# Late attention scores from rounded parts, one PSUM bank for two early results, layer 1 started four slots earlier, products three steps behind

## The chip, the cores and the metric

The kernel runs on one core of a Trainium2 chip. The time is that of the whole program in device microseconds (us), median of three runs. Engines are called as the profile calls them: PE is TensorE (PEld its weight loads), DVE is VectorE, ACT is ScalarE, POOL is GpSimd, and SP is the engine whose queue issues nearly all DMAs.

## The reference

Block-causal attention (4 batches, 8 heads, 576 positions of 64 values, blocks of 64), whose output goes through two feed-forward layers.

```python
scores = scale * np.matmul(q, k.transpose(0, 1, 3, 2))
mask = block_i >= block_j
scores = np.where(mask, scores, -1000000000.0)
scores = scores - np.max(scores, axis=-1, keepdims=True)
attn = np.exp(scores)
attn = attn / (np.sum(attn, axis=-1, keepdims=True) + 1e-09)
x = np.matmul(attn, v)                        # to (2304, 512)
h = x @ w_in                                  # 512 -> 2048, layer 1
x = (np.maximum(h, 0.0) + alpha * np.minimum(h, 0.0)) @ w_out
h = x @ w_in2                                 # layer 2
y = np.where(h > 0.0, h, np.exp(np.minimum(h, 0.0)) - 1.0) @ w_out2
```

Here `scale` is 0.125. Everything is 32-bit on input and output.

## The kernel before

**Pairs and slots.** Two heads of one batch make a pair; there are 16. A pair's 576 queries are cut into tiles: queries 0 to 255 are one early tile (i = 0), and 256 to 383, 384 to 511 and 512 to 575 (of both heads) are the late tiles i = 2, 3 and 4. The attention runs in 64 slots, one tile in each, in an order written out by hand: slots 0 to 15 are the early tiles of pairs 0 to 15, slots 16 to 63 the late tiles, three slots a pair. In slot k `scores` puts q times k of its tile in one of two double banks of PSUM (`pair`), `maxima` takes the row maxima on DVE (with a memset for the mask), and `exponentials` runs Exp on ACT. Two slots on `normalise` scales the tile `p` by the reciprocal of its sums, on POOL; three slots on (early) or five (late) PE transposes it and ACT and DVE copy it to `pt`; five (early) or seven slots on `second` multiplies it with v, and ACT and DVE write the result to `x` as a rounded part and the rest. Each engine works through its list in the order in which the program was written, so an instruction that waits holds all behind it on its engine.

**Two kinds of product.** A 32-bit product on PE runs as two instructions in the profile. Elsewhere the kernel takes a number apart into a high part rounded to the matmul's fp32r format and the low rest, and sums three fp32r products, high by high, high by low and low by high (`PASSES`). Before the change the scores are 32-bit products, layers 1 and 2 are threefold fp32r products. The two heads of a pair lie in partitions 0 to 63 and 64 to 127, and their score products use the two halves of the array; tile i = 4 takes both heads at once through `qdiag`, a 128 by 128 block-diagonal matrix of q.

**PSUM banks.** Transposes and the results of `second` take banks in turn from the ring `t`, banks 4 to 7. Once layer 1 begins beside attention the ring has banks 4 to 6, and bank 7 alone holds layer 1's sums (ring `h`).

**Layer 1 beside attention.** Tokens are in five units (512, 512, 512, 512, 256). For units 0 to 2 the first four of 16 slices of the hidden dimension are computed during attention by `l1_beside`: 16 parts of six products each, for every unit first 8 parts of h = x w_in (L523), then 8 of h w_out (L534). The parts are strewn between slots: unit 0 over slots 18 to 33, unit 1 to 47, unit 2 to 71. After the second part of each h, `l1_gate` takes Relu on ACT (`neg`), g on DVE in the next slot behind that slot's maxima, the rounded part on ACT and the rest on POOL (tile `gs`). The weights come as 64-bit halves of 512 KB through `load_w`, which converts them with two ACT, three DVE, a POOL, an ACT and a DVE instruction; slots in `w_slots` start one.

**Afterwards** the rest of layer 1 (units in stages A, B, D) and layer 2 (stage C) run step by step: step i computes h for one slice (L505, L556), and behind it come the output products (L606, L581) of step i - `lag`, with `lag` = 2. g and e have two buffers (tag `g`), h has three banks, the sums have five.

## Time and profile before

| what | value |
|---|---|
| time, median of 3 runs | 1034.4 us (1034.02 to 1036.47) |
| the profiled execution | 1030.47 us, span 1028.7 us, mean granted PE clock 0.988 |
| PE busy | 971.9 us (94%), 4912 matmuls |
| DVE, ACT, POOL busy | 542.3 (53%), 432.4 (42%), 291.6 us (28%) |
| chain that ended last | PE 65%, DVE 11%, DMA 10%, ACT 4%, POOL 4% |

The profiled execution is 0.4% under the median. Busy shares are over the whole span; attention with layer 1 beside it is the first 275 us, where all engines are much in use, and the rest is mostly PE.

### The profile page before, as it was taken

The page shows a single profiled execution, that of the slowest core. Times are in us where ns is not written, and L with a number is a line of the kernel's source. Part 1 is how long each engine was busy: PE and PEld are TensorE (multiplying, and loading weights), DVE is VectorE, ACT ScalarE, POOL GpSimd, SP SyncE. Part 2 cuts the span into 40 slices and gives each one's busy share as a digit, 9 for nine tenths or more (in the row PEclk, how much of TensorE's full clock was granted, in tenths as well). Part 3 has the DMA queues.
Part 4 walks back from the last instruction along what each step waited for, and adds up shares of the span by engine and source line. Part 5 has one row for each costly group of instructions (what it writes and reads, how often), then busy time and mean ns, then how long its engine had stood idle before and what let it go on. Part 6 is the DMA issues. An engine that isn't in the chain of part 4 may idle for free.

```text
span 1028.7 us, 13713 instructions
## 1 busy us (share of the span) xinstructions
PE 971.9 (94%) x4912; PEld 766.2 (74%) x4912; DVE 542.3 (53%) x1070; ACT 432.4 (42%) x953; POOL 291.6 (28%) x344
## 2 busy tenths in 40 slices
PE   6778999999989999999999998999999999999997
PEld 4445666666667877779888886788888888888896
DVE  6886566677476776753213378833333333333343
ACT  6775565576355554543223355422222222222232
POOL 3555254345255545443323344300000000000000
PEclk8999999999989999999999999999999999999999
DMA  6454352633536677545523255202100200200010
GB/s 211 154 200 141 89 143 76 209 103 115 200 107 201 221 234 217 180 155 185 164 82 123 105 191 222 98 1 83 41 1 7 117 1 1 83 1 1 1 42 21
DMA packets 61156, 116.25 MB, mean 113 GB/s; under 512 B 11552, under 2 KB 29984, under 8 KB 59936
## 3 DMA queue, kind: packets, MB, share of 16 engines
q1 hardware_dynamic: 60800, 115.11, 34.2%
q8 instruction: 39, 0.64, 0.3%
q10 hardware_dynamic: 288, 0.26, 0.1%
q14 instruction: 29, 0.24, 0.1%
HBM read 83.89 MB, written 31.46 MB: 112 GB/s over the span
## 4 chain that ended last, share of the span: by engine, by line
PE 65%; DVE 11%; DMA 10%; ACT 4%; issue 4%; POOL 4%; SPq 0%; POOLq 0%; ACTq 0%; DVEq 0%
PE bank L581 18%; PE bank L556 17%; DMA wraw<-w 8%; PE bank L606 6%; PE bank L505 6%; PE bank L390 4%; PE pair L249 3%; POOL wword L142 3%; PE bank L523 3%; PE bank L534 3%; PE bank L336 2%; DVE wword L137 2%; DVE wword L132 2%; DVE wword L133 2%; ACT wword L127 2%
## 5 line engine op out<-in xcount | busy, mean ns | idle before, releaser
L556 PE MATMUL bank<-x,w 128*128 128x512 f32 (+1 forms) x960 | 210.0, 368 | 0.0
L556 PEld LDWEIGHTS bank<-x,w 128*128 128x128 f32 x960 | 169.3, 188 | 31.3
L505 PE MATMUL bank<-x,w 128*128 128x512 f32 (+1 forms) x816 | 175.7, 365 | 1.3 <-DVE xtail L83 1.3
L505 PEld LDWEIGHTS bank<-x,w 128*128 128x128 f32 x816 | 141.5, 189 | 26.1 <-ACT xtail L396 1.4
L561 DVE TENSOR_SCALAR e<-e 128x512 f32<-128x512 f32 (+1 forms) x80 | 31.9, 399 | 172.0 <-ACT e L560 172.0
L560 ACT ACTIVATE e<-bank 128x512 f32<-128x512 f32 (+1 forms) x80 | 44.3, 554 | 184.8 <-PE bank L556 184.8
L142 POOL TENSOR_TENSOR wword<-wword,wraw 128x512 int32<-128x512 int32 x64 | 91.6, 1432 | 91.5 <-DVE wword L137 45.4
L488 DVE SCALAR_TENSOR_TENSOR g<-neg,beta,bank 128x512 f32<-128x512 f32 (+1 forms) x80 | 55.2, 690 | 105.6 <-ACT neg L485 103.6
L581 PE MATMUL bank<-w,gsl 128*128 128x512 f32 x432 | 105.9, 391 | 2.6 <-DVE z L617 1.3
L581 PE MATMUL bank<-w,gs 128*128 128x512 f32 x432 | 105.0, 390 | 1.0 <-DVE gs L83 1.0
L90 POOL TENSOR_SCALAR p<-p,stat 128x128 f32<-128x128 f32 (+4 forms) x144 | 78.0, 555 | 92.1 <-DVE stat L307 69.2
L606 PE MATMUL bank<-gsl,w 128*128 128x512 f32 (+1 forms) x408 | 93.6, 375 | 9.4 <-ACT gsl L492 3.5
L581 PEld LDWEIGHTS bank<-w,gsl 128*128 128x128 f32 x432 | 80.3, 188 | 20.7 <-DVE z L617 2.1
L581 PEld LDWEIGHTS bank<-w,gs 128*128 128x128 f32 x432 | 80.5, 188 | 17.8 <-DVE gs L83 1.5
L83 POOL TENSOR_TENSOR gs<-g,gs 128x512 fp32r<-128x512 f32 (+1 forms) x46 | 58.9, 1280 | 120.5 <-ACT gs L492 113.8
L606 PE MATMUL bank<-gs,w 128*128 128x512 f32 (+1 forms) x408 | 89.1, 366 | 3.0 <-POOL gs L83 3.0
L606 PEld LDWEIGHTS bank<-gsl,w 128*128 128x128 f32 x408 | 71.9, 193 | 26.0 <-ACT gsl L492 4.1
L298 ACT ACTIVATE p<-pair,stat 128x128 f32<-128x128 f32 (+4 forms) x144 | 78.3, 557 | 30.8 <-DVE stat L281 29.0
L606 PEld LDWEIGHTS bank<-gs,w 128*128 128x128 f32 x408 | 70.5, 189 | 16.6 <-POOL gs L83 4.5
L485 ACT ACTIVATE neg<-bank 128x512 f32<-128x512 f32 (+1 forms) x80 | 43.9, 549 | 72.5 <-PE bank L505 69.2
L83 DVE TENSOR_TENSOR w<-wword,w 128x512 fp32r<-128x512 f32 x64 | 58.3, 915 | 26.6 <-ACT w L152 25.6
L270 DVE TENSOR_REDUCE stat<-pair 128x2 f32<-128x256 f32 (+3 forms) x80 | 63.2, 806 | 7.7 <-PE pair L254 5.7
(68 smaller groups left out, 1174.0 us busy)
## 6 DMA issues: line engine op xcount, KB each, us to landing
wraw<-w SPq DMA_DIRECT2D x64, 512.0 KB, 4.1
x<-xd SPq DMA_DIRECT2D x24, 512.0 KB, 6.9
xd<-x SPq DMA_DIRECT2D x4, 2048.0 KB, 7.7
x<-yd SPq DMA_DIRECT2D x4, 2048.0 KB, 8.7
vraw<-v_a SPq DMA_DIRECT2D x24, 256.0 KB, 3.7
zd<-z SPq DMA_DIRECT2D x20, 256.0 KB, 2.8
kraw<-kT SPq DMA_DIRECT2D x16, 288.0 KB, 4.0
yd<-gsl SPq DMA_DIRECT2D x8, 512.0 KB, 4.1
```

Of the source, the lines that this page charges most:

```text
L83: return {"v": dve, "p": pool_e}[eng].tensor_tensor(out=out, in0=x, in1=f32(high), op=ALU.subtract)
L90: return pool_e.tensor_scalar(out, x, 1.0 if scale is None else scale, 1.0, ALU.mult, ALU.mult)
L142: pool_e.tensor_tensor(out=w, in0=w, in1=units, op=ALU.add)
L270: peak = lambda out, x, axis=AX.X: dve.tensor_reduce(out=out, in_=x, axis=axis, op=ALU.max, negate=True)
L298: act.activation(out=out, in_=x, func=AF.Exp, bias=stat[:, k:k + 1], scale=0.125, accum_out=stat[:, SUMS + 2 * k:SUMS + 2 * k + 1])
L485: act.activation(out=neg, in_=h, func=AF.Relu, scale=-1.0)
L488: dve.scalar_tensor_tensor(out=g, in0=neg, scalar=beta[:, f:f + 1], in1=h, op0=ALU.mult, op1=ALU.add)
L505: pe.matmul(h, w_in(0, f, wp_, kc), x[:, xp_, kc, :n], start=kc == 0 and t == 0, stop=kc == KC - 1 and t == 2)
L556: pe.matmul(h, w_in(1, f, wp_, kc), x[:, xp_, kc, :], start=kc == 0 and t == 0, stop=kc == KC - 1 and t == 2)
L560: act.activation(out=e, in_=h, func=AF.Exp)
L581: pe.matmul(acc, gs[:, gp_, tg * P:(tg + 1) * P], w_out(1, f, wp_, 0, DM), start=f == 0 and t == 0, stop=f == NF - 1 and t == 2)
L606: pe.matmul(acc, w_out(0, f, wp_, m * P, P), gs[:, gp_, :n], start=first and t == 0, stop=last and t == 2)
```

## The change

1. Early tiles: q is multiplied by 0.125 in place, once for two pairs (POOL, 128 by 512; the first on DVE in two halves), and the multiplication of the maxima (L281) and the scale of Exp go.
2. Late tiles: `high_parts` (POOL: q times 0.125 rounded, 128 by 320; k rounded, and k minus that, 128 by 576 each), three slots before the pair's first late slot; `low_parts` (one DVE instruction of 128 by 320), two before; `diagonal` fills two matrices, the rounded one on POOL, the low one on ACT. The scores are threefold fp32r products.
3. The result of `second` for an early tile and the smaller of the early tile's two groups of transposes share one bank, so an early slot takes two banks of the ring, not three.
4. Layer 1 beside attention starts at slot 14: unit 0's h parts lie in slots 14 to 22 and its output parts in 22 to 30, unit 1's in 30 to 39 and 39 to 47, unit 2's in 47 to 59 and 59 to 71. The first weight half starts in slot 1 instead of before slot 0, and eight are started by slot 16 instead of 18.
5. `lag` is 3, and g and e have three buffers.

```diff

-    qdiag = [ap1.tile([P, P], F32, name=f"qdiag{i}") for i in range(2)]
-    for t in qdiag:
-        pool_e.memset(t, 0.0)
+    qdiag = [[ap1.tile([P, P], F32R, name=f"qdiag{i}{k}") for k in range(2)] for i in range(2)]
+    for ts in qdiag:
+        for t in ts:
+            pool_e.memset(f32(t), 0.0)

...
         b, p = PAIRS[n]
-        st[n]["q"], st[n]["k"] = q, k = raw_tiles()
+        st[n]["raw"] = q, k = raw_tiles()
         hs = slice(2 * p, 2 * p + 2)
...

+    def high_parts(n):
+        s = st[n]
+        q, k = s["raw"]
+        for which, x, scale in (("q", q[:, 256:], 0.125), ("k", k, None)):
+            s[which] = [ap2.tile([P, x.shape[1]], F32R, tag=f"{which}{t}", name=f"{which}{t}") for t in "hl"]
+            copy("p", s[which][0], x, scale)
+        low_part("p", s["k"][1], k, s["k"][0])
+
+    def low_parts(n):
+        s = st[n]
+        hi, lo = s["q"]
+        dve.scalar_tensor_tensor(out=lo, in0=s["raw"][0][:, 256:], scalar=0.125, in1=f32(hi), op0=ALU.mult, op1=ALU.subtract)
+
     def diagonal(n):
-        for x in range(2):
-            r = slice(64 * x, 64 * x + 64)
-            copy("p", qdiag[n % 2][r, r], st[n]["q"][r, 512:])
+        for low in range(2):
+            for x in range(2):
+                r = slice(64 * x, 64 * x + 64)
+                copy("pa"[low], qdiag[n % 2][low][r, r], f32(st[n]["q"][low])[r, 256:320])

...
         if i < 4:
-            c = 256 * (n % 2) if i == EARLY else 0
-            tiles = [(c + P * j, slice(lo, hi)) for j, lo, hi in EARLY_TILES] if i == EARLY else [
-                (P * i, slice(0, P * (i + 1)))]
-            for q0, cols in tiles:
+            if i == EARLY:
+                c = 256 * (n % 2)
+                for j, lo, hi in EARLY_TILES:
+                    for x in range(2):
+                        r = slice(64 * x, 64 * x + 64)
+                        pe.matmul(sb[:, x, lo:hi], s["q"][r, c + P * j:c + P * j + P], s["k"][r, c:c + hi - lo],
+                                  start=True, stop=True)
+                return
+            q0, cols = P * i - 256, slice(0, P * (i + 1))
+            for t, (qp, kp) in enumerate(PASSES):
                 for x in range(2):
                     r = slice(64 * x, 64 * x + 64)
-                    pe.matmul(sb[:, x, cols], s["q"][r, q0:q0 + P], s["k"][r, c:c + cols.stop - cols.start],
-                              start=True, stop=True)
+                    pe.matmul(sb[:, x, cols], s["q"][qp][r, q0:q0 + P], s["k"][kp][r, cols], start=t == 0, stop=t == 2)
         else:
...
             for r in range(2):
-                pe.matmul(sb[:, r, :kn], qdiag[n % 2], s["k"][:, kn * r:kn * (r + 1)], start=True, stop=True)
+                for t, (qp, kp) in enumerate(PASSES):
+                    pe.matmul(sb[:, r, :kn], qdiag[n % 2][qp], s["k"][kp][:, kn * r:kn * (r + 1)],
+                              start=t == 0, stop=t == 2)

...
             peak(stat[:, 0:1], sb[:, :, :S // 2], AX.XY)
-        dve.tensor_scalar(stat[:, :width(i)], stat[:, :width(i)], 0.125, None, ALU.mult)

...
         for k, (out, x) in enumerate(todo):
-            act.activation(out=out, in_=x, func=AF.Exp, bias=stat[:, k:k + 1], scale=0.125,
+            act.activation(out=out, in_=x, func=AF.Exp, bias=stat[:, k:k + 1],
                            accum_out=stat[:, SUMS + 2 * k:SUMS + 2 * k + 1])
...
             for t, lo, hi in EARLY_TILES:
-                tb, w = bank[take("t")], hi - lo
+                tb, w = (shared.pop() if shared and t == 0 else bank[take("t")]), hi - lo
                 for x in range(2):
...

+    shared = []
+
     def second(n, half):
...
         chunks = range(2 if half == 0 else 5)
-        op = bank[take("t")]
+        if half == 0:
+            shared[:] = [bank[take("t")]]
+            op = shared[0][:, 256:]
+        else:
+            op = bank[take("t")]
         for j in chunks:
...

-    transposes_at, products_at, other_at = {}, {}, {}
+    transposes_at, products_at, other_at, SPLITS = {}, {}, {}, {}

...
         plan(k + 7, lambda n=n: second(n, 1), products_at)
+    def scale_early(d, cols, eng):
+        q = st[2 * d]["q"][:, cols]
+        copy(eng, q, q, 0.125)
+
     for d in range(1, NP // 2):
+        plan(2 * d - 2, lambda d=d: scale_early(d, slice(0, 512), "p"))
         if d > 1:
...
         plan(k - 6, lambda n=n: load_late(n))
+        plan(k - 3, lambda n=n: high_parts(n), SPLITS)
+        plan(k - 2, lambda n=n: low_parts(n))
         plan(k - 1, lambda n=n: diagonal(n))
...
             scores(*here)
+        shared.clear()
         outs = [p() for p in products_at.get(k, ())]
         move = transposes(*transposes_at[k]) if k in transposes_at else None
+        for emit in SPLITS.get(k, ()):
+            emit()
         for emit in NORM.get(k, ()):
...
         neg = gp.tile([P, 512], F32, tag="neg", name="neg", bufs=1)[:, :n]
-        g = gp.tile([P, 512], F32, tag="g", name="g", bufs=2)[:, :n]
+        g = gp.tile([P, 512], F32, tag="g", name="g", bufs=3)[:, :n]
         t = gs_tile()[:, :, :n]
...
                           start=kc == 0 and t == 0, stop=kc == KC - 1 and t == 2)
-        e = gp.tile([P, 512], F32, tag="g", name="e", bufs=2)[:, :n]
+        e = gp.tile([P, 512], F32, tag="g", name="e", bufs=3)[:, :n]
         gs = gs_tile()[:, :, :n]
...
         load_early(1)
+        for half in range(2):
+            scale_early(0, slice(256 * half, 256 * half + 256), "v")
         load_early_v(0)
-        load_w(*halves.pop(0))
         load_alpha()
...
         end_tick()
-        LEAD = 18
-        ends = [33, X_DONE[2], LAST]
-        w_slots = {3, 6, 9, 12, 14, 16, 18}
+        LEAD = 14
+        stretches = [(LEAD, 22, 22, 30), (30, 39, 39, X_DONE[2]), (X_DONE[2], 59, 59, LAST)]
+        w_slots = {1, 3, 6, 8, 10, 12, 14, 16}
         w_slots |= {27 + 5 * i for i in range(8)}
...
                 if k in w_slots:
-                    arrival[0] = 4 if k > 20 else 2
+                    arrival[0] = 4 if k > 21 else 2
                     load_w(*halves.pop(0))
...
         k = LEAD
-        for u, end in enumerate(ends):
-            assert k >= X_DONE[u]
-            parts, n, first = l1_beside(u), 2 * (FA + KC), k
-            for j in range(n):
-                next(parts)
-                to = first + (2 * (j + 1) * (end - first) + n) // (2 * n)
-                slots(k, to)
-                k = to
+        for u, (a, b, c, d) in enumerate(stretches):
+            assert a >= X_DONE[u]
+            parts = l1_beside(u)
+            for first, end, n in ((a, b, 2 * FA), (c, d, 2 * KC)):
+                slots(k, first)
+                k = first
+                for j in range(n):
+                    next(parts)
+                    to = first + (2 * (j + 1) * (end - first) + n) // (2 * n)
+                    slots(k, to)
+                    k = to
         arrival[0] = 2
...
             first_of.setdefault((k, u), i)
-        lag = 2
+        lag = 3
         w_at = {}
```

On PE at slots 14 to 16, before the change (L249 is a score product, L390 the product with v, L329 a transpose; bank_106 is bank 7):

```order
L249 MATMUL pair_101<-kraw,qraw 128x128 x2
L249 MATMUL pair_101<-kraw,qraw 128x256 x2
L390 MATMUL bank_106<-pt,vraw_113 64x256 x2
L390 MATMUL bank_106<-pt,vraw_113 64x128 x2
L329 MATMUL bank_103<-ident,p_568 128x128 x2
L329 MATMUL bank_104<-ident,p_568 128x128 x4
L249 MATMUL pair_102<-kraw,qraw 128x128 x2
L249 MATMUL pair_102<-kraw,qraw 128x256 x2
L390 MATMUL bank_105<-pt,vraw_114 64x256 x2
L390 MATMUL bank_105<-pt,vraw_114 64x128 x2
L329 MATMUL bank_106<-ident,p_608 128x128 x2
L329 MATMUL bank_103<-ident,p_608 128x128 x4
```

And the same place with the change, up to the scores of slot 16 (L560 is a part of layer 1's h, L270 a late score product, kh, kl, qh and ql the rounded and low parts):

```order
L560 MATMUL bank_106<-x_318,w 128x512 x6
L263 MATMUL pair_102<-kraw,qraw 128x128 x2
L263 MATMUL pair_102<-kraw,qraw 128x256 x2
L417 MATMUL bank_105<-pt,vraw_114 64x256 x2
L417 MATMUL bank_105<-pt,vraw_114 64x128 x2
L350 MATMUL bank_105<-ident,p_613 128x128 x2
L350 MATMUL bank_103<-ident,p_613 128x128 x4
L560 MATMUL bank_106<-x_318,w 128x512 x6
L270 MATMUL pair_101<-kh,qh 128x384 x2
L270 MATMUL pair_101<-kl,qh 128x384 x2
L270 MATMUL pair_101<-kh,ql 128x384 x2
```

Parts of layer 1 now stand ahead of slots 15 and 16, the product with v and the first transposes go to the same bank, and three score products stand where one 32-bit product of two instructions stood.

On POOL around slots 13 to 16 before (L90 p is a normalisation, L142 a weight's addition, L90 qdiag the diagonal):

```order
L90 TENSOR_SCALAR p_525<-p_525,stat_123 128x128 x2
L90 TENSOR_SCALAR p_525<-p_525,stat_123 128x256 x2
L142 TENSOR_TENSOR wword<-wword,wraw 128x512
L90 TENSOR_SCALAR p_568<-p_568,stat_124 128x128 x2
L90 TENSOR_SCALAR p_568<-p_568,stat_124 128x256 x2
L90 TENSOR_SCALAR p_608<-p_608,stat_119 128x128 x2
L90 TENSOR_SCALAR p_608<-p_608,stat_119 128x256 x2
```

And with the change:

```order
L90 TENSOR_SCALAR qraw<-qraw 128x512
L90 TENSOR_SCALAR qh<-qraw 128x320
L90 TENSOR_SCALAR kh<-kraw 128x576
L83 TENSOR_TENSOR kl<-kraw,kh 128x576
L90 TENSOR_SCALAR p_573<-p_573,stat_128 128x128 x2
L90 TENSOR_SCALAR p_573<-p_573,stat_128 128x256 x2
L142 TENSOR_TENSOR wword<-wword,wraw 128x512
L90 TENSOR_SCALAR p_613<-p_613,stat_123 128x128 x2
L90 TENSOR_SCALAR p_613<-p_613,stat_123 128x256 x2
L142 TENSOR_TENSOR wword<-wword,wraw 128x512
```

The three instructions of `high_parts` stand ahead of a slot's normalisation, behind the scaling of the last early q.

On PE at the start of stage A before (L505 is h of a step, L606 the output products of an earlier one):

```order
L505 MATMUL bank_2675<-x_2023,w 128x512 x12
L505 MATMUL bank_2676<-x_2023,w 128x512 x12
L505 MATMUL bank_2677<-x_2023,w 128x512 x12
L606 MATMUL bank_2670<-gsl,w 128x512 x3
L606 MATMUL bank_2671<-gsl,w 128x512 x3
```

And with the change (L542 and L643 are the same lines of code):

```order
L542 MATMUL bank_2976<-x_2249,w 128x512 x12
L542 MATMUL bank_2977<-x_2249,w 128x512 x12
L542 MATMUL bank_2978<-x_2249,w 128x512 x12
L542 MATMUL bank_2976<-x_2249,w 128x512 x12
L643 MATMUL bank_2971<-gsl,w 128x512 x3
L643 MATMUL bank_2972<-gsl,w 128x512 x3
```

A fourth h, in the bank of the first, now stands ahead of the first output products, and so it goes on to the end of layer 2.

## Rows read from the trace of the kernel before

**Rows 1.** Windows: stretch, its length, busy time (instructions) by engine, PE clock, DMA.

```profile
0.00:52.18 52.18, 35.37 (x251) 22.71 (x251) 39.25 (x113) 36.44 (x136) 24.64 (x64) 0.87 0.60 187
52.18:67.82 15.64, 12.00 (x86) 7.29 (x87) 13.23 (x37) 13.04 (x44) 7.62 (x19) 1.00 0.66 221
67.82:198.49 130.67, 118.62 (x665) 77.66 (x664) 86.16 (x224) 74.09 (x186) 58.07 (x88) 0.99 0.39 119
198.49:275.26 76.77, 73.76 (x457) 47.92 (x457) 54.17 (x150) 48.35 (x122) 35.57 (x51) 1.00 0.45 142
275.26:1028.70 753.44, 732.15 (x3456) 610.60 (x3456) 349.50 (x549) 260.50 (x468) 165.72 (x125) 0.99 0.30 102
```

**Rows 2.** Waits of PE, 0 to 52.18 us: total, times, longest.

```profile
PE bank L329 <- DVE x L83: 5.0, 4, 1.6
```

**Rows 3.** Waits of PE, 67.82 to 275.26 us.

```profile
PE bank L523 <- DVE g L488: 8.0, 4, 3.7
```

**Rows 4.** Waits of PE, 275.26 us to the end.

```profile
PE bank L606 <- ACT gsl L492: 3.5, 2, 3.0
...
PE bank L581 <- DVE gsl L83: 0.5, 1, 0.5
```

**Rows 5.** Timeline of PE: start, length, line, output and inputs, count [idle before].

```profile
136.81 1.13 PE L254 MATMUL pair<-kraw,qdiag 128*128 128x288 f32 x4
137.77 0.82 PE L336 MATMUL bank<-ident,p 128*128 128x128 f32 x6
...
139.90 0.92 PE L249 MATMUL pair<-kraw,qraw 64*128 64x384 f32 x4
140.74 2.42 PE L390 MATMUL bank<-pt,vraw 128*64 128x320 f32 x20
...
145.50 1.13 PE L249 MATMUL pair<-kraw,qraw 64*128 64x512 f32 x4
146.56 0.66 PE L342 MATMUL bank<-ident,p 128*128 128x128 f32 x4
```

**Rows 6.** Timeline of PE at the start of stage A.

```profile
275.26 8.42 PE L505 MATMUL bank<-x,w 128*128 128x512 f32 x36 [1.27 <-DVE xtail L83]
286.67 0.79 PE L606 MATMUL bank<-gsl,w 128*128 128x512 f32 x1 [2.98 <-ACT gsl L492]
288.02 5.06 PE L606 MATMUL bank<-gsl,w 128*128 128x512 f32 x11 [0.56 <-POOL gsl L83]
292.88 2.42 PE L505 MATMUL bank<-x,w 128*128 128x512 f32 x9
```

**Rows 7.** Timeline of ACT in that stretch.

```profile
280.88 0.67 ACT L128 ACTIVATE wraw<-wraw 128x512 int32<-128x512 uint32 x1 [6.35 <-DMA wraw<-w]
```

**Rows 8.** Timeline of POOL in that stretch.

```profile
285.01 1.26 POOL L83 TENSOR_TENSOR gs<-g,gs 128x512 fp32r<-128x512 f32 x1 [9.66 <-ACT gs L492]
...
288.25 1.41 POOL L83 TENSOR_TENSOR gsl<-g,gsl 128x512 fp32r<-128x512 f32 x1 [0.28 <-ACT gsl L492]
```

**Rows 9.** Timeline of DVE in that stretch.

```profile
286.31 0.75 DVE L488 SCALAR_TENSOR_TENSOR g<-neg,beta,bank 128x512 f32<-128x512 f32 x1 [2.02 <-POOL gs L83]
287.17 3.04 DVE L83 TENSOR_TENSOR w<-wword,w 128x512 fp32r<-128x512 f32 x2
```

**Rows 10.** Groups by line and shape, 0 to 275 us: busy, mean ns, idle before.

```profile
L83 POOL TENSOR_TENSOR gs<-g,gs 128x512 fp32r<-128x512 f32 x12 | 16.0, 1333 | 36.2 <-ACT gs L492 36.1
...
L83 DVE TENSOR_TENSOR w<-wword,w 128x512 fp32r<-128x512 f32 x16 | 12.1, 757 | 2.3 <-ACT w L152 2.3
...
L90 POOL TENSOR_SCALAR p<-p,stat 128x576 f32<-128x576 f32 x16 | 11.9, 746 | 15.8 <-DVE stat L307 12.2 <-DVE pair L277 3.6
...
L281 DVE TENSOR_SCALAR stat<-stat 128x4 f32<-128x4 f32 x16 | 6.1, 383 | 0.6
```

**Rows 11.** Timeline of SP: the late load of pair 6.

```profile
116.10 0.42 SPq L221 DMA_DIRECT2D kraw<-kT  x1
```

**Rows 12.** DMA issues of the page: KB each, us to landing.

```profile
kraw<-kT SPq DMA_DIRECT2D x16, 288.0 KB, 4.0
```

## The prediction

> **What bounds the kernel now.** I read the busy time by stretch first, cut where the program changes: slot 14 begins at 52.18, slot 18 at 67.82, slot 47 at 198.49, and the first product of stage A at 275.26 [rows 1]. From slot 18 to stage A PE is busy 118.62 + 73.76 = 192.4 of 207.4 us, and after that 732.15 of 753.44: PE is the bound from slot 18 on, with 15.1 and 21.3 us of idle time in its row. Before slot 14 it isn't: PE works 35.37 of 52.18 us, DVE 39.25, ACT 36.44, and in slots 14 to 17 DVE 13.23 and ACT 13.04 of 15.64. There a slot is the sum of hand-overs between two nearly full engines. So time comes from three places: PE work that goes, PE idle time that is filled, and early slots that grow or shrink.
>
> The waits of PE name the idle time. In the early slots it is the transposes that wait for DVE to empty a bank, 5.0 us in four times [rows 2]; from slot 18 it is layer 1's h, which waits for g to be read out of its only bank, 8.0 us [rows 3]; in the stages it is the output products that wait for `gs`, in five rows of the view that come to 9.2 us, of which the first and the last are shown [rows 4]; the rest there are waits for DVE to empty sums, which the change leaves alone.
>
> **Late scores.** From start to start the 32-bit scores take 0.96 us (i = 4), 0.84 (i = 2) and 1.06 (i = 3) [rows 5]. The first is 4 instructions of 288 columns, 0.24 each, or 0.83 ns a column. The 64-row tiles have 4 instructions too, but 4 times 384 columns at that rate would be 1.28, so the two heads run beside each other: two deep 0.64, and 0.20 that doesn't stream; for i = 3 0.85 and 0.21. A threefold fp32r product of full height costs 8.42 / 36 = 0.23 us for 512 columns [rows 6], about 0.13 for 288 and 0.16 of streaming for 384. If the heads still run side by side and the 0.20 is paid once a tile, i = 4 becomes 6 x 0.13 = 0.80 (-0.16), i = 2 becomes 0.48 + 0.20 (-0.16), i = 3 0.64 + 0.21 (-0.21): -0.53 a pair, **-8.5** over 16. No row shows fp32r on 64 rows. Lower bound: nothing but streaming, 0.48, 0.64 and 0.80, -0.94 a pair, -15.0. Upper bound: the heads one behind the other, 6 x 0.17 = 1.04 and 6 x 0.23 = 1.36, +0.34 a pair, +5.4. I take the value nearest to how the same tiles run now.
>
> **The splits.** POOL gets per pair a copy of 576 columns, 0.75, one of 320, 0.41 by the same row, and a subtraction of 576, 1.33 x 576/512 = 1.50 [rows 10]: 2.7 us. In the fullest stretch, slot 47 on, POOL works 35.57 of 76.77 [rows 1]; its six pairs or so there add 16, so it stands at some 70%. A normalisation behind the splits has three slots until its transposes in late slots, so it is late for nobody. DVE gets one low part, 0.75 x 320/512 = 0.47 by the g instruction [rows 9], and loses three scalings of maxima; ACT gets two copies of 64 by 64. All of it lies under PE's work; without that cover it would be 2.7 us a pair. The splits read k three slots sooner than the products did. Pair 6's load was issued at 116.10 and takes 4.0 [rows 11, 12], so it lands near 120, and was used at 139.90 [rows 5]; three slots are 3 x 130.67 / 29 = 13.5 us, which leaves 6 us. I put it at 0.
>
> One cost can't be bounded away: DVE and POOL disturb each other. While POOL subtracted at 288.25 [rows 8], two subtractions of weights on DVE took 3.04 us [rows 9], which is 1.5 each against a mean of 0.76 [rows 10]. By the trace that is 0.75 us for each such meeting, and DVE, 54.17 of 76.77 in its fullest stretch [rows 1], has room for that. The Trainium skill (SBUF — State Buffer, Terms) has it that the pair is an exclusive lock for a whole instruction, and that the loser "fully blocks". Taken at its word, any of DVE's instructions with two SBUF inputs could wait out a whole POOL instruction; that is a rival below.
>
> **Early slots, 0 to 13.** DVE loses a scaling of 0.38 us in every slot [rows 10], 5.4 us in all, and the 5.0 us of waits for banks [rows 2] should go, since an early slot takes two banks of four. Against it stand two scalings of q on DVE ahead of the first scores, and one to two more weight halves that now fall ahead of slot 14, on DVE and ACT. DVE's saving about pays for the halves, ACT's share rises. I take **-1**, bounds -4 and +3.
>
> **Slots 14 to 17.** One part of layer 1 stands there now, ahead of slot 18; with the change there are four, each 6 x 0.23 = 1.4 us, so PE goes from 12.00 to 16.2 us in a stretch of 15.64, while DVE takes on two g's and two low parts and ACT two Relus. The fullest engine works 13.23 of 15.64 us, 85% [rows 1]; at that share 16.2 needs 19.1: +3.5, while 4.2 of PE work is gone from behind slot 18: **-0.7**. Bounds: -4.2 if it all fits in, +3 if a slot here loses 1.5 us more to hand-overs.
>
> **Idle time from slot 18 to stage A.** Of its 15.1 us, 8.0 are h waiting for its bank [rows 3], all in the slots in which DVE also converts weights. Half of unit 0's h parts have moved to earlier slots, the weights are through two slots sooner, and unit 1 has 17 slots for its 16 parts instead of 14. I take **-6**; bounds 0 (the wait moves along with the parts) and -10.
>
> **Three steps behind.** Stage A's 36 first products take 8.42 us from 275.26, and the next h begins at 292.88 [rows 6]. At 0.23 us the 48 products until then need 10.9, so 6.7 are lost: ACT, in order, waited until 280.88 for a weight to land [rows 7] before it could take Relu of the first h, so `gs` came from POOL at 285.01 + 1.26 [rows 8], and eleven of the output products behind it ran at 5.06 / 11 = 0.46 us each [rows 6]. With `lag` 3 PE has four h's, 10.9 us, before it needs that `gs`, until 286.2; it is ready at 286.3. The fourth h wants the bank of the first, which g has read by 283 or so. So nearly all of the 6.7 goes. Of the 9.2 us of waits for `gs` 2.98 and 0.56 lie here, and the other 5.7 are short single waits; a step more of slack, 24 products or 5.4 us, covers each. DVE's wait of 2.02 for a g buffer [rows 9] goes with the third buffer. 12.4 in all; I take **-11** for what turns up anew, bounds -4 and that 12.4. What is late next are the sums that DVE empties between units, which stay.
>
> **Sum.** -8.5 - 1 - 0.7 - 6 - 11 = -27.2, against the profiled execution's 1030.47 (span 1028.7): 1003. The median stands 3.9 us above that execution; with the same difference it is 1034.4 - 27.2 = **1007**.
>
> **Rivals.**
> A. The fp32r halves don't overlap: +5.4 in place of -8.5, 1021. For it: no row shows them. Against: the same partitions and banks overlap now.
> B. The landing of a weight holds ACT longer at stage A, and the fourth h waits for its bank as the output products did: the first 6.7 stay, 1014. For it: an idle time of 6.35 us before one ACT instruction. Against: only 3 us more would matter.
> C. The blocked port: three of DVE's two-input instructions a pair each lose 0.8 us to a POOL instruction. A pair is 207.4 / 16 = 13 us now, of which DVE works 71% in its fullest stretch; 2.4 more and the low part's 0.47 would bring it to 12.1 us, as long as PE's work, and the gain from slot 18 on (8.5 + 6) is lost: 1022. By the lock of that page this would come; the rows show the delay, but few meetings.
> D. It ends slower: POOL waits for landings. Each pair's splits stand in POOL's list ahead of normalisations and `gs`, and if loads land late POOL stands still for that time in every pair. With the change a pair is about 13 - 14.5 / 16 = 12.1 us, of which POOL works 35.57 / 76.77 of 13, or 6.0, and 2.7 more, so a wait of up to 3.4 costs nothing; 5.1 a pair makes the pair 1.7 = 27.2 / 16 longer and takes all the gain. At 6.0 the median would be 1034.4 + 16 x 0.9 = 1049. For it: SP issues in order, behind stores that wait. Against: 6 us of room in the load shown.
> E. Several of these at once, within 0.3%.
>
> **Chances.** Forecast 0.57 (its own range 998 to 1017, from the bounds of the terms), A 0.13, B 0.10, C 0.08, D 0.07, E 0.05. A measurement of this kernel can tell 0.3%, 3 us, from no change. Faster: 0.57 + 0.13 + 0.10 + 0.08 = 0.88; same 0.05; slower 0.07. The range goes from 994, where the score, idle and early terms reach their lower bounds (6.5 + 4 + 3 more), to 1023, which takes in A, B and C and leaves out D, E and the ends of the forecast.
>
> **What would show it.** Late scores from start to start at 0.68, 0.85 and 0.80, and the two heads' instructions starting in pairs; slot 14 near 51, slot 18 near 70, stage A's first product near 259; h's waits for g about 3 us; the next h after stage A's first output products without a gap, and waits for `gs` of about 1 us in all the stages; POOL near 70% from slot 47 on. Wrong would be: six score instructions in a row in 1.0 us or more (A), a PE gap after the third or fourth h of stage A (B), DVE near 95% in late slots (C), POOL idle on a DMA of k (D), or slots 14 to 17 of 6 us, which would eat what the earlier start brings.

## The result and the profile after

The changed kernel takes 1019.37 us (median, 1017.45 to 1023.51) beside 1034.21 for the kernel before on the same chip: ratio 0.9858, interval 0.9821 to 0.9896, so 14.8 us faster. That lies in the predicted range of 994 to 1023, but 12 us above the predicted 1007 and 2 us outside the forecast's own 998 to 1017. The profiled execution took 1017.45 us with a span of 1015.7, 13.0 less than before's 1028.7, and the account below is made between these two.

Windows of the changed kernel, cut as in [rows 1]: slot 14 begins at 50.86, slot 18 at 73.70, slot 47 at 189.01, stage A at 264.40.

```profile
0.00:50.86 50.86, 35.82 (x256) 22.59 (x256) 37.08 (x100) 37.91 (x138) 30.30 (x73) 0.97 0.60 187
50.86:73.70 22.84, 17.31 (x109) 11.47 (x109) 18.05 (x44) 16.57 (x51) 19.88 (x31) 0.93 0.60 218
73.70:189.01 115.31, 107.94 (x699) 77.49 (x698) 80.93 (x196) 73.37 (x198) 76.39 (x110) 0.99 0.38 120
189.01:264.40 75.39, 71.09 (x492) 50.47 (x491) 56.10 (x136) 51.81 (x134) 47.86 (x65) 1.00 0.47 151
264.40:1015.70 751.30, 731.39 (x3456) 612.87 (x3456) 351.29 (x549) 260.50 (x468) 163.05 (x125) 0.99 0.30 102
```

Slots 0 to 13 take 1.3 us less than in [rows 1], slots 14 to 17 take 22.84 instead of 15.64, slot 18 to stage A 190.70 instead of 207.44, and the stages 751.30 instead of 753.44. So the gain is made between slot 18 and stage A, part of it is paid back in slots 14 to 17, and the stages, where the largest term of the prediction lay, give 2.1. Of the 16.7 us between slot 18 and stage A, 6.4 are four parts of layer 1 that now stand ahead of slot 18 (three in slots 14 to 17, one at the end of slot 13), and PE's idle time is 11.67 us instead of 15.05.

PE's timeline at late scores (to set against [rows 5]) and at the start of stage A ([rows 6]):

```profile
236.21 0.44 PE L270 MATMUL pair<-kh,qh 64*128 64x384 f32 x2
236.49 0.34 PE L270 MATMUL pair<-kl,qh 64*128 64x384 f32 x2
236.66 0.34 PE L270 MATMUL pair<-kh,ql 64*128 64x384 f32 x2
236.93 2.42 PE L417 MATMUL bank<-pt,vraw 128*64 128x320 f32 x20
...
241.68 0.50 PE L270 MATMUL pair<-kh,qh 64*128 64x512 f32 x2
...
242.58 0.66 PE L363 MATMUL bank<-ident,p 128*128 128x128 f32 x4
...
243.10 0.38 PE L275 MATMUL pair<-kh,qdiag 128*128 128x288 f32 x1
...
243.98 0.82 PE L357 MATMUL bank<-ident,p 128*128 128x128 f32 x6
...
264.40 11.16 PE L542 MATMUL bank<-x,w 128*128 128x512 f32 x48 [1.27 <-DVE xtail L83]
275.40 0.39 PE L643 MATMUL bank<-gsl,w 128*128 128x512 f32 x1
276.39 2.79 PE L643 MATMUL bank<-gsl,w 128*128 128x512 f32 x11 [0.61 <-POOL gsl L83]
279.02 2.88 PE L542 MATMUL bank<-x,w 128*128 128x512 f32 x12
```

From start to start the scores take 0.72 (i = 2), 0.90 (i = 3) and 0.88 us (i = 4; 0.80 to 0.89 over the pairs): 0.12, 0.16 and 0.08 to 0.16 less than before. The two heads' products start in pairs, within 0.01 us of each other. At stage A the four h's run through, and about 0.9 us is lost ahead of the next h where it was 6.7.

Waits of PE from there to the end (total, times, longest), which answer to [rows 4]:

```profile
PE bank L643 <- ACT z L87: 5.3, 1, 5.3
PE bank L643 <- DVE z L650: 4.8, 3, 2.3
PE bank L643 <- DVE zl L89: 1.6, 2, 0.9
PE bank L643 <- DVE zl L650: 1.4, 2, 1.1
...
PE bank L643 <- POOL gsl L83: 0.6, 1, 0.6
```

The 9.2 us of waits for `gs` are down to 0.6. In their place the output products of layer 1 wait 13.1 us for sums (`z`, `zl`) to be emptied. Before, the same waits came to 4.4, nearly all of it in these two rows:

```profile
PE bank L606 <- DVE z L613: 2.5, 3, 1.4
PE bank L606 <- DVE zl L613: 1.7, 2, 1.1
```

The longest of the new waits stands here in PE's timeline, and behind it ACT's and SP's in the same stretch:

```profile
313.32 1.60 PE L542 MATMUL bank<-x,w 128*128 128x256 f32 x12
314.76 0.52 PE L643 MATMUL bank<-gsl,w 128*128 128x256 f32 x3
320.63 1.01 PE L643 MATMUL bank<-gsl,w 128*128 128x256 f32 x3 [5.35 <-ACT z L87]
...
324.15 2.55 PE L542 MATMUL bank<-x,w 128*128 128x256 f32 x12
```

```profile
315.63 0.40 ACT L529 CAST gs<-g 128x256 fp32r<-128x256 f32 x1 [0.87 <-DVE g L525]
317.36 0.66 ACT L127 ACTIVATE wword<-wraw 128x512 f32<-128x512 f32 x1 [1.32 <-DMA wraw<-w]
...
318.60 0.67 ACT L127 ACTIVATE wword<-wraw 128x512 f32<-128x512 f32 x1
...
319.72 0.39 ACT L522 ACTIVATE neg<-bank 128x256 f32<-128x256 f32 x1
319.98 0.59 ACT L87 COPY z<-bank 128x512 f32<-128x512 f32 x1
```

```profile
303.99 3.18 SPq L507 DMA_DIRECT2D x<-xd  x4
309.75 4.44 SPq L117 DMA_DIRECT2D wraw<-w  x2
```

The last products of unit 3 end at 313.5, its first sum was complete even sooner. The copy to z that empties this sum's bank began at 319.98, because in ACT's list two weight halves and a Relu stand ahead of it, and ACT, in order, stood idle for the 1.32 us before 317.36 until the first half landed. That half was issued at 309.75, behind the four loads of the next x, and landed 7.5 us later; the median of these loads is 4.1. PE also loses clock: it is idle from 315.3, the granted clock is 0.50 (the lower level, 1.2 GHz) from 319.5 to 326.3, and the twelve products at 324.15 take 2.55 us instead of 1.60.

The other waits for sums have DVE in ACT's place. It is mostly at work on weights there rather than idle, and in front of five of these waits a bit operation on a weight (L133), 0.43 us as a rule, takes 1.40 to 1.45. One of the five, in PE's and DVE's timelines:

```profile
377.32 3.98 PE L643 MATMUL bank<-gsl,w 128*128 128x512 f32 x9 [1.83 <-DVE z L650]
```

```profile
374.49 1.45 DVE L133 TENSOR_SCALAR wword<-wword 128x512 uint32<-128x512 uint32 x1
...
376.58 0.68 DVE L650 TENSOR_TENSOR z<-bank,z 128x512 f32<-128x512 f32 x1
```

What makes L133 longer is in the last section.

### The profile page after: what moved, and what is told of

Read it like the earlier page. It is cut to its first block, busy times and chain, and to the rows that moved or that the text cites. A ratio compares the mean times of both kernels' runs of the same rounds, so it can differ in the third digit from the quotient of the medians.

```text
span 1015.7 us, 13946 instructions
## 1 busy us (share of the span) xinstructions
PE 963.5 (95%) x5008; PEld 774.9 (76%) x5008; DVE 543.4 (54%) x1024; ACT 440.2 (43%) x985; POOL 337.5 (33%) x401
## 4 chain that ended last, share of the span: by engine, by line
PE 68%; DVE 11%; DMA 9%; POOL 4%; ACT 4%; issue 2%; SPq 1%; POOLq 0%; ACTq 0%; DVEq 0%
PE bank L618 19%; PE bank L593 18%; PE bank L643 9%; PE bank L542 8%; DMA wraw<-w 6%; PE bank L417 3%; POOL wword L142 3%; PE bank L571 3%; DVE wword L137 2%; PE bank L357 2%; PE pair L270 2%; PE bank L560 2%; DVE wword L133 2%; DVE wword L132 2%; ACT wword L127 1%
## 5 line engine op out<-in xcount | busy, mean ns | idle before, releaser
L542 PE MATMUL bank<-x,w 128*128 128x512 f32 (+1 forms) x816 | 176.7, 367 | 1.3 <-DVE xtail L83 1.3
L542 PEld LDWEIGHTS bank<-x,w 128*128 128x128 f32 x816 | 142.7, 191 | 26.2 <-ACT xtail L423 1.4
L142 POOL TENSOR_TENSOR wword<-wword,wraw 128x512 int32<-128x512 int32 x64 | 89.8, 1405 | 92.5 <-DVE wword L137 53.8
L643 PE MATMUL bank<-gsl,w 128*128 128x512 f32 (+1 forms) x408 | 94.6, 379 | 13.7 <-ACT z L87 5.3
L90 POOL TENSOR_SCALAR p<-p,stat 128x128 f32<-128x128 f32 (+4 forms) x144 | 81.3, 579 | 53.9 <-DVE stat L328 43.4
L643 PEld LDWEIGHTS bank<-gsl,w 128*128 128x128 f32 x408 | 72.8, 196 | 30.0 <-DVE z L650 6.3
L643 PE MATMUL bank<-gs,w 128*128 128x512 f32 (+1 forms) x408 | 87.8, 364 | 0.0
L643 PEld LDWEIGHTS bank<-gs,w 128*128 128x128 f32 x408 | 70.6, 189 | 12.2
L83 DVE TENSOR_TENSOR w<-wword,w 128x512 fp32r<-128x512 f32 x64 | 61.0, 957 | 24.5 <-ACT w L152 23.7
```

The source lines that it names most:

```text
L83: return {"v": dve, "p": pool_e}[eng].tensor_tensor(out=out, in0=x, in1=f32(high), op=ALU.subtract)
L90: return pool_e.tensor_scalar(out, x, 1.0 if scale is None else scale, 1.0, ALU.mult, ALU.mult)
L142: pool_e.tensor_tensor(out=w, in0=w, in1=units, op=ALU.add)
L542: pe.matmul(h, w_in(0, f, wp_, kc), x[:, xp_, kc, :n], start=kc == 0 and t == 0, stop=kc == KC - 1 and t == 2)
L643: pe.matmul(acc, w_out(0, f, wp_, m * P, P), gs[:, gp_, :n], start=first and t == 0, stop=last and t == 2)
```

## The experiments

All thirteen times, each as a ratio to the kernel before in its own comparison, with its interval, and the span of its profiled execution:

| kernel | ratio | span, us |
|---|---|---|
| changed | 0.9858 [0.9821, 0.9896] | 1015.7 |
| lag 2 | 0.9878 [0.9861, 0.9895] | 1018.7 |
| start at slot 18 | 0.9901 [0.9885, 0.9918] | 1020.1 |
| 32-bit late scores | 0.9924 [0.9910, 0.9938] | 1024.6 |
| before with lag 3 | 0.9982 [0.9970, 0.9994] | 1031.5 |
| normalisation first | 0.9870 [0.9848, 0.9892] | 1020.3 |
| hand order | 0.9837 [0.9815, 0.9860] | 1015.5 |
| weights' work cut | 0.9781 [0.9758, 0.9803] | 1010.9 |
| third raw buffer | 0.9924 [0.9900, 0.9947] | 1024.7 |
| hand order, A and B | 0.9748 [0.9731, 0.9765] | 1005.8 |
| the same, lag 2 | 0.9806 [0.9787, 0.9826] | 1011.7 |
| two halves later | 0.9890 [0.9870, 0.9911] | 1020.7 |
| g first | 0.9743 [0.9712, 0.9774] | 1007.5 |

0.001 is 1.03 us. The changed kernel's own interval is 4 us wide to either side, so what differs from it by less is read from stretches of the traces. Its profiled execution is the fastest of its four runs, 1.9 us under their median, so a difference of spans can be that much larger than one of ratios for a slower kernel, and that much smaller for a faster one.

**1. The parts alone.** Four kernels. The scaled early q and the shared bank had no run of their own.

```diff
-        lag = 3
+        lag = 2
```

> The changed kernel with the output products two steps behind the first ones again instead of three (the third g buffer stays). First theory: three steps behind removed the 9 us of waits for gs, but waits for the sums between units took their place, so the step was worth about 2 us: 1.5 to 3 us slower than the changed kernel (about 1021), with the waits for gs back at 8 to 10 us and the waits for z down from 13 us to about 4. Rival: the step is worth the 11 us of the prediction and the missing gain is elsewhere: 9 to 12 us slower (about 1029).

```diff
-        LEAD = 14
-        stretches = [(LEAD, 22, 22, 30), (30, 39, 39, X_DONE[2]), (X_DONE[2], 59, 59, LAST)]
-        w_slots = {1, 3, 6, 8, 10, 12, 14, 16}
+        LEAD = 18
+        ends = [33, X_DONE[2], LAST]
+        w_slots = {3, 6, 9, 12, 14, 16, 18}
...
```

> The changed kernel with layer 1 beside attention beginning at slot 18 again, with the old stretches and the old slots for the weight loads. First theory: the start at slot 14 costs 7 us in slots 14 to 17 and gives back about 9 from slot 18 to stage A, so that it is worth 2 to 3 us together with the 1 us ahead of slot 14: the kernel without it is 2 to 4 us slower (about 1022), slots 14 to 17 take 14 to 16 us again. Rival 1: it is worth the 7.7 us of the prediction: 1027. Rival 2: it costs more than it gives back, and the kernel without it is 2 to 5 us faster (about 1015).

```diff
-            for t, (qp, kp) in enumerate(PASSES):
-                for x in range(2):
-                    ...
-                    pe.matmul(sb[:, x, cols], s["q"][qp][r, q0:q0 + P], s["k"][kp][r, cols], start=t == 0, stop=t == 2)
+            q, k = s["raw"]
+            for x in range(2):
+                ...
+                pe.matmul(sb[:, x, :P * (i + 1)], q[r, P * i:P * i + P], k[r, :P * (i + 1)], start=True, stop=True)
...
-        plan(k - 3, lambda n=n: high_parts(n), SPLITS)
-        plan(k - 2, lambda n=n: low_parts(n))
...
```

> The changed kernel with its late scores in 32 bits again, without the splits on POOL, DVE and ACT; everything else as changed. First theory: the shorter scores are worth what their start to start differs, 0.46 us a pair or 7.4 us, and the splits are hidden: 6.5 to 8.5 us slower than the changed kernel (about 1027). Rival: the splits hold up DVE and POOL in the slots in which layer 1's gates and the weights are converted, and eat half of it or more: 0 to 4 us slower (1019 to 1023), with the waits for g and p of slots 18 to 63 down from 10 us to below 6.

The fourth is the kernel before with `lag = 3` and `bufs=3` for g and e.

> The kernel before with the output products three steps behind and three g buffers; nothing else. First theory: about 2 us faster than before (1032), the waits for gs gone and waits for sums between units of 10 us or more in their place. Rival, the prediction's term: 9 to 12 us faster (about 1024).

Lag 2 is 0.0020 above the changed kernel, less than the intervals tell apart, with 7.2 us of waits for `gs` and `gsl` in A, B and D back (8 to 10 had been expected) and those for z and zl there at 4.7. Alone on the kernel before, three steps gain 1.9 us (0.6 to 3.1), and the same waits arise there:

```profile
PE bank L606 <- DVE z L613: 5.3, 3, 2.5
PE bank L606 <- ACT z L87: 5.1, 1, 5.1
```

So the step is worth about 2 us in either kernel, and the rival of 11 falls. The 32-bit scores cost 6.8 us by the ratios; a late pair's three slots, where PE waits for nothing and two parts of layer 1 stand between in both, take 10.36 us with them and 9.90 without, 0.46 x 16 = 7.4. From slot 18 to stage A the 32-bit kernel is only 5.6 us longer, since PE is idle for 10.01 us in it instead of 11.67. So the splits cost at most about 1.7 us there, and the rival, by which they eat half or more, falls on the 6.8 and the 7.4, though the interval of the ratios alone wouldn't exclude it. The start at slot 18 costs 4.4 us: there slot 18 to stage A takes 201.06 us, 10.4 more than with the start at 14 (4.3 of it is idle time of PE, the rest the four parts of layer 1 that then lie there), slots 14 to 17 take 20.08, 2.8 less, and slots 0 to 13 take 48.87, 2.0 less. The first theory expected 14 to 16 us for slots 14 to 17, and that was wrong: even with almost no layer 1 in them they grew by 4.4 over [rows 1]. The waits of PE in them, with the start at 18, point to the splits, since the early normalisations stand behind them on POOL:

```profile
PE bank L350 <- POOL p L90: 4.3, 4, 1.9
```

**2. Slots 14 to 17.** First the order on POOL:

```diff
-        for emit in SPLITS.get(k, ()):
-            emit()
         for emit in NORM.get(k, ()):
             emit()
+        for emit in SPLITS.get(k, ()):
+            emit()
```

> The changed kernel with the normalisations ahead of the splits in POOL's list, in every slot; nothing else. First theory: the splits of pairs 0 and 1 fall in slots 13 and 16, where early normalisations stand behind them that are wanted one slot later, and the chain runs over POOL there: 1.5 to 4 us faster than the changed kernel (about 1016.5), slots 14 to 17 at 19 to 21 us instead of 22.84. Rival: as predicted, nobody waits for POOL behind the splits, slots 14 to 17 are held by DVE and ACT: within 1 us of the changed kernel.

The slots take 22.84 us, as in the changed kernel, and the ratio is 0.9870: the rival held. The 32-bit kernel has no splits at all, and its slots 14 to 17 take 24.34, though its DVE has more to do there (21.32 us against 18.05). With the start at 14 the order of POOL's list isn't what makes these slots long. Then two weight halves out of these slots, `w_slots = {1, 3, 6, 8, 10, 12, 17, 18}`:

> The changed kernel with the two weight halves that are loaded at slots 14 and 16 loaded at slots 17 and 18. First theory: DVE holds slots 14 to 17, and each half costs it 2.3 us there: the four slots shrink from 22.84 us by 3 to 5, and slots 18 to 22 grow by about as much, since DVE is as full there: within 2 us of the changed kernel in all. Rival: PE and the splits make these slots long: they stay at 22 us or more.

They take 22.87 us, while slots 18 to 21 take 22.10 instead of 17.36, and the kernel is 3.3 us slower. The rival's number held; but the conversions that now lie later belonged to slot 16 and after, so of what DVE does in slots 14 and 15 this says nothing. What these slots wait for in the changed kernel is seen in PE's timeline, and below it in DVE's:

```profile
53.94 0.87 PE L417 MATMUL bank<-pt,vraw 128*64 128x256 f32 x8 [2.15 <-DVE pt L89]
...
55.37 1.64 PE L560 MATMUL bank<-x,w 128*128 128x512 f32 x6
...
62.23 1.90 PE L560 MATMUL bank<-x,w 128*128 128x512 f32 x6 [2.75 <-DVE g L525]
```

```profile
57.09 0.56 DVE L243 SCALAR_TENSOR_TENSOR ql<-qraw,qh 128x320 fp32r<-128x320 f32 x1
...
60.49 1.02 DVE L292 TENSOR_REDUCE stat<-pair 128x2 f32<-128x256 f32 x2
61.43 0.74 DVE L525 SCALAR_TENSOR_TENSOR g<-neg,beta,bank 128x512 f32<-128x512 f32 x1
```

The first h is complete at 57.0, g frees its only bank at 62.2, behind 4 us of other work in DVE's list, and the next h holds up the scores behind it in PE's. The last experiment of the series takes g ahead of the maxima (it builds on the hand order of part 3):

```diff
-        if here:
-            maxima(*here)
         after = [h() for h in held]
         held.clear()
+        if here:
+            maxima(*here)
```

> The kernel with ACT's and DVE's lists in the order of the code through the A and B units, and beside attention each g on DVE ahead of the maxima of its slot instead of behind them; nothing else. First theory: what is left of idle time between slot 14 and stage A, 12 us in seven waits of h and of the first output products for g (8.1 and 3.6), comes from g's place in DVE's list, behind 1.2 us of maxima: the seven waits lose about 1 us each, slots 14 to 17 come below 22 us, 3 to 7 us faster than that kernel (about 1003). Rival: the maxima are what the next slots wait for, and g waits for ACT anyway: the waits move to the scores and the transposes, within 2 us or slower.

The waits of h and of the first output products for g fall from 11.7 to 4.9 us, but the slots still take 22.84, with 2.1 us of transposes that wait for POOL and a longer slot 17; the time is the same. The rival held, and ACT's timeline shows one reason. DVE begins the first g at 59.65 instead of 61.43, but ACT's rounding of it stands behind the exponentials of slot 15 and begins when it did, here in the changed kernel and in this one:

```profile
63.34 0.64 ACT L529 CAST gs<-g 128x512 fp32r<-128x512 f32 x1
```

```profile
63.37 0.63 ACT L529 CAST gs<-g 128x512 fp32r<-128x512 f32 x1
```

POOL waits for it and begins the rest of g at 64.06 and 64.08, and behind it in POOL's list stand the splits and the normalisation that slot 17's transposes need. So what DVE's list gives up doesn't get past ACT's and POOL's.

**3. The sums in the stages.** Five kernels test why they are late. In the stages the program fixes the order of PE's list alone; the lists of ACT, DVE and POOL are ordered by the scheduler.

```diff
-    with tc.manual_schedule(engines={ET.PE}):
+    with tc.manual_schedule(engines={ET.PE, ET.Activation, ET.DVE}):
```

> The changed kernel with ACT's and DVE's instructions in the stages in the order in which the code issues them (the scheduler orders only PE's list by hand as it stands); the same instructions, but the emptying of a sum stands behind at most one weight half instead of two. First theory: sums wait for their emptying because it stands in ACT's and DVE's lists behind weights that have just landed or not landed yet; with the other order the waits for z in the A and B units fall from 13 us to below 6, and the kernel is 5 to 9 us faster than the changed one (about 1012). Rival: with three steps behind the two engines have too little time for the sums whatever the order: the waits only move, within 2 us of the changed kernel or slower.

```diff
-            act.activation(out=units, in_=low, func=AF.Copy, scale=2.0 ** -29)
+            if not plain:
+                act.activation(out=units, in_=low, func=AF.Copy, scale=2.0 ** -29)
...
+            if plain:
+                dve.tensor_scalar(w, w, 1.0, 0.001, ALU.min, ALU.mult)
+                return
...
-        later(lead + 1, sign)
-        later(lead + 2, rounded)
+        if not plain:
+            later(lead + 1, sign)
+            later(lead + 2, rounded)
```

(`plain` holds for layer 1's weights in the stages.)

> The changed kernel with a part of the conversion of layer 1's last eight chunks left out in the stages (one of ACT's two reads of the raw words, DVE's sign and POOL's addition; what is left is replaced by a bound and a factor), so that the numbers that come out are other ones. First theory: it is the conversion that holds the emptying of sums: stage waits for z fall from 13 us to below 4, 8 to 12 us faster than the changed kernel (about 1009). Rival: the sums are late for another reason (the bank ring, the stores): z waits stay above 8 us, within 4 us.

```diff
-        raw = wraw_p.tile([P, 2 * DM], U32, tag="wraw", name="wraw")
+        n_w[0] += 1
+        wp, nb = (late_pools[0], 1) if late_pools and n_w[0] % 3 == 0 else (wraw_p, 2)
+        raw = wp.tile([P, 2 * DM], U32, tag="wraw", name="wraw", bufs=nb)
...
-        return late_pools[0].tile([P, 2, 512], F32R, tag="gsl", name="gsl", bufs=4)
+        return late_pools[0].tile([P, 2, 512], F32R, tag="gsl", name="gsl", bufs=3)
```

> The changed kernel with a third buffer for a raw weight half and its word in the stages (and three gsl buffers instead of four, to make room). First theory: the loads of weights are issued only when POOL has added up the half two before, and land behind the loads of x; with a third buffer they are issued some 5 us sooner and ACT no longer stands at a weight that has not landed: the 5.35 us ahead of the emptying of unit 3's sums goes, 3 to 6 us faster (about 1015). Rival: the instructions themselves, not the landing, hold the emptying: within 2 us.

In hand order the A and B units have not one wait of 0.3 us for a sum, but stage C has 11.1 us of waits where it had 0.8 (layer 2's h waits for DVE to read its bank into `e`, 5.3 in five times), so it comes out 2.2 us below the changed kernel, less than the intervals tell apart, between the two theories. Cutting the weights' work gains 8.0 us by the ratios and 4.8 by the spans, and yet the waits for sums stay at 11.5: the longest is 6.41 us, and ACT's rows in front of it are these, with the wait for the landing grown to 4.24:

```profile
319.25 0.66 ACT L127 ACTIVATE wword<-wraw 128x512 f32<-128x512 f32 x1 [4.24 <-DMA wraw<-w]
319.81 0.66 ACT L129 ACTIVATE wraw<-wraw 128x512 int32<-128x512 uint32 x1
```

L129 is the read that the edit leaves out of layer 1's weights, so this weight is one of layer 2's, and whole. The scheduler puts ten halves of layer 2 ahead of stage D. The gain lies behind the A and B units: from D's first product to C's first it takes 197.26 us instead of 202.84, and from A's first to D's first 140.73, no less than in the changed kernel. So less conversion doesn't help the sum that stands behind a load that hasn't landed; this run doesn't say what less conversion of those very weights would do. The third raw buffer gave no answer: with it and one `gsl` less the scheduler's lists came out otherwise, one wait of 7.2 us for a sum arose in C, and it is 6.8 us slower. Then the hand order for A and B alone:

```diff
+    with tc.manual_schedule(engines={ET.PE, ET.Activation, ET.DVE}):
...
+        for i in range(31):
+            step(i)
+
+    with tc.manual_schedule(engines={ET.PE}):
+        for i in range(31, len(steps) + lag):
+            step(i)
```

> The changed kernel with ACT's and DVE's lists in the order of the code up to the end of the A and B units only; the units D and C, where that order had brought new waits of 14 us, are left to the scheduler. First theory: the waits for sums of the A and B units, 10 us (the five of 0.3 us or more up to 402, and what the clock loses behind them), go, and nothing else changes: 7 to 11 us faster than the changed kernel (about 1010). Rival: the waits turn up again later, as they did in C: within 3 us.

> The same with the output products two steps behind. First theory: with the sums emptied in time the third step is worth what the prediction put it at, the waits for gs that it removes: 5 to 9 us slower than the one with three steps (about 1017). Rival: the waits for gs were a matter of ACT's order too, and two steps do as well in that order: within 2 us of the one with three.

With three steps it takes 1007.77 us, 0.0110 or 11.4 us below the changed kernel and 26.1 below the kernel before; it and the one with g first, which builds on it, are the fastest here. ACT's timeline at the same place as above:

```profile
310.94 0.58 ACT L87 COPY z<-bank 128x512 f32<-128x512 f32 x1
311.69 0.59 ACT L87 COPY z<-bank 128x512 f32<-128x512 f32 x1 [0.18 <-PE bank L643]
312.18 0.68 ACT L127 ACTIVATE wword<-wraw 128x512 f32<-128x512 f32 x1
```

The copies of the sums stand ahead of the weight, and PE has no wait there. From stage A's first product to D's first it takes 125.89 us instead of 140.08. But two more things differ in that stretch. ACT takes up 16 weight halves there instead of 24, since those of layer 2 are left for the stages behind; and no L133 is lengthened there, where eight were. So the order of the two lists is what gains; how much of it is the place of the emptying, how much the eight halves and how much the meetings with POOL, these runs don't separate. From there to C's first product it gives 4.9 back, in one wait for a sum between D's first two units, behind two weight halves in DVE's list, so that expectation's "nothing else changes" was too simple:

```profile
453.98 1.01 PE L643 MATMUL bank<-gsl,w 128*128 128x256 f32 x3 [5.92 <-DVE z L654]
```

With two steps in the same order the stretch from A to D takes 128.57 us, against 141.82 for two steps in the scheduler's order, and the whole is 0.0058 or 6.0 us slower, of which the traces show 4.1 from stage A on. So the order takes away the waits for `gs` in A and B too, at two steps all but 1.4 us at stage A's start; the third step is worth 4 to 6 us once the order is right, and about 2 in the scheduler's.

## Why the prediction came out as it did

The direction and the range held, the middle was 12 us too low. That the range held was in part luck: the time lies outside the forecast's own 998 to 1017, and what takes it in is the room that the range left for A, B and C, none of which came in the way that was described. By its own terms, between the two profiled executions:

| term | predicted | measured | how |
|---|---|---|---|
| late scores | -8.5 | -7.4 | 16 x 0.46 |
| slots 0 to 13 | -1 | -1.3 | start of slot 14; the 5.0 of [rows 2] are gone |
| slots 14 to 17 | -0.7 | +0.8 | +7.2, less 6.4 of work gone from behind slot 18 |
| idle time, slot 18 to A | -6 | -3.4 | PE's idle time, 15.05 to 11.67 |
| three steps behind | -11 | -2.1 | stage A to the end |
| sum | -27.2 | -13.4 | spans: -13.0 |

(The median stands 1.9 us above the profiled execution, not 3.9 as the prediction took over from before; that is 2 us of the miss in the other direction.)

**Three steps behind** is the step that was mis-sized, by 9 us. Its mechanism was right as far as it went: the four h's cover the first `gs`, the 6.7 us at stage A became 0.9, and the 9.2 us of waits for `gs` became 0.6. Wrong was the sentence that what is late next, the sums that DVE empties between units, "stay". In the view behind [rows 4] they were a rest of 4.4 us, and I took a small wait for slack. It was small because PE came late: as soon as PE no longer waited for `gs`, it reached the bank of the sum while ACT and DVE were still at, or idle for, the weights in front of it. Going from two steps to three takes these waits from 4.4 to 13.4 us on the kernel before, and going back takes them from 13.1 to 4.7 on the changed one. The order of ACT's and DVE's lists then gives 9.7 us from stage A to the end with the same instructions. [rows 7] held the hint, ACT idle for 6.35 us on a landing, and the prediction used it for one place only.

**Slots 14 to 17** were the second miss, +7.2 in place of +3.5, hidden in the table because four parts of layer 1, 6.4 us, have gone from behind slot 18 and not three: PE's work there came to 17.31 us rather than 16.2, part of it at a lower clock (0.93), and 5.5 us of waits for DVE stand on top. The growth rate from one engine's busy share (85%) was too kind for slots in which three engines hand over to each other and h has one bank. That the slots might take 6 us each was named as what would eat the early start; slots 14 and 15 take 6.08 and 7.12, and against the start at 18 these slots and the ones ahead of them give back 4.8 of the 10.4 us. What bounds them was not settled, beyond the chain from DVE's g over ACT's rounding to POOL that held when g came first: without splits, with the normalisations first, with weights later and with g first they took 24.34, 22.84, 22.87 and 22.84 us.

**Splits at 0**: right for the late slots; POOL works 47.86 of 75.39 us from slot 47 on, 63%, where 70% was forecast. It was wrong in its reason: slots 13 and 16 still hold early normalisations, wanted one slot later and not three, and with the start at slot 18 PE waits 4.3 us for them. With the start at 14 PE doesn't wait for them; that the waits for DVE hide it is likely, not shown.

**Scores**: right within 1.1 us; the 0.16 us of streaming for 384 columns stands in no row, 0.23 us for 512 gives 0.17. **Idle time**: 3.4 of the 6. The waits of h for g between slot 18 and stage A fell from 8.0 [rows 3] to 4.8, not to 3, and those of the output products for g are 3.7. Rival A fell on the pairs, B on the four h's that run through, D on the late slots: none of PE's waits for POOL there is of 0.3 us or more. C did not come in the late slots: DVE stands at 56.10 of 75.39, 74%. But its mechanism, DVE held by POOL, came up in the stages, ahead of the sums.

## What to carry to other kernels

A wait that is small in a profile is not slack: it can be small because the waiting engine came late. Before a wait is priced away, follow the next one in the same engine's list as if the first were gone, and read which instruction stands ahead of its releaser. In an engine's list one instruction that waits for a load holds everything behind it, so short work that frees a bank belongs ahead of work that waits for data. Here a different order of two engines' lists, which also held later weights back, was worth more (11.4 us) than the whole change of distance (about 2).

## What the runs showed of the hardware

DVE and POOL meet in one-input instructions too. In the changed kernel's DVE timeline the bit operation on a weight (L133) takes 1.40 us beside an addition of POOL that had begun 0.37 us sooner:

```profile
423.88 1.40 DVE L133 TENSOR_SCALAR wword<-wword 128x512 uint32<-128x512 uint32 x1
```

```profile
423.51 1.49 POOL L142 TENSOR_TENSOR wword<-wword,wraw 128x512 int32<-128x512 int32 x1
```

The median of its 64 executions is 0.427 us and the longest is 1.509; it ends 0.28 after POOL's. Of the 64, 15 met a two-input POOL instruction that had begun sooner, and all 15 end 0.28 or 0.29 after that one's end, after 0.85 to 1.51 us; of six in which POOL began later five took their usual 0.42 or 0.43, one 0.81. That agrees with the Trainium skill (SBUF — State Buffer, Who interferes with whom), by which a `tensor_scalar` can be one of those DVE instructions that take the port pair shared with GpSimd, and whoever issues first gets the pair for the whole instruction. The prediction counted only two-input meetings. Five of the 15 stand right in front of a sum on which PE then waited, 6.4 us in all; as each is about 1 us longer than usual, they make an estimated 4 of that. No run takes them away alone.

fp32r products on 64 rows run side by side for two heads as 32-bit ones do, but not at the rate of full-height products: three pairs of 384 columns take 0.72 us, where three products at that rate, 0.23 us for 512 columns in [rows 6], would take 0.52.
